# A tuned attention and gated-layer kernel: a first pass over x without the low half, and the first gates placed ahead of the rest of the first layer

## The chip, the cores and the metric

The kernel runs on one core of a Trainium2 chip. The metric is device time in microseconds (us), the median of several executions. Before the change it was 775.09 us (median of 3, 774.56 to 775.32). A profile gives times from the start of its own span, which is some 2 us shorter than the device time.

## The reference, cut to what matters

Two steps on x of 4 batches, 12416 rows, 128 columns. First attention through 32 inducing vectors, twice: the inducing vectors look at x, then x looks at the result `h`. Then a gated feed-forward layer on each row.

```python
def mab(q, kv):                      # attention; scale = 1/sqrt(128)
    a = softmax(scale * q @ kv.T)
    return a @ kv
h = mab(I, x)                        # 32 x 128 per batch
y = mab(x, h)                        # 12416 x 128 per batch
g = y @ w_gate                       # 128 -> 1536
ffn = gelu(g) * (y @ w_val) @ w_out
out = y + sigmoid(y @ w_res) * ffn
```

Since y is a mix of only 32 rows of `h`, the kernel multiplies `h` with the gate and value weights first (called the first layer, `hgv`). A gate is then a product of the attention weights `rt` (32 rows) with `hgv`, followed by a GELU on ScalarE.

## The kernel before: the parts that the change and the argument touch

The first batch has nothing to hide behind: its whole x has to be read before `h`, and `h` is needed for the first gate. Its first pass takes 13 tiles of 1024 rows (the last one short). Each tile is cast to fp16 (`hi`), transposed on TensorE, multiplied with the inducing vectors, put through exp, and summed into the accumulator `acc`, weighted with the exps. In most tiles x is summed as a pair of fp16 numbers, a high and a low half; in five (`whole`) as fp32, as it was loaded.

```python
    for n in range(ntile + 2):
        hi_next(n + 1)                                  # cast of the next tile
        if n < ntile:
            if tiles[n] not in whole:
                convert_lo(0, tiles[n], ve)             # VectorE: x - hi
            turn_pe(0, tiles[n], ve if n in (9, 11, 12) else act)
        if 1 <= n <= ntile:
            ...
            exps("a", 0, n0, n0 + w, bank_v())          # scores and exps
        if n >= 2:
            ...
            if tiles[n - 2] in whole:
                sum_whole(n0, w, n == ntile + 1)        # sums of the exps, VectorE
            accumulate(0, n0, n0 + w, n == 2, n == ntile + 1)
```

Then comes the way from the accumulator to the first gate:

```python
    turn_first_h(0)                       # accumulator -> ht, h transposed
    ...                                   # exps "b": x looks at h, blocks 0 to 32
    exps("b", 0, WIDE, 2 * WIDE, bank_v())          # scores 32 to 64
    exps("b", 0, *later[0], bank_g())
    weights_b(0, 0, 0, half, ve, True)
    first_layer(0, 0, layers[:, :TOK])              # two products, then a VectorE copy
    for j in later[1:]:
        exps("b", 0, *j, bank_g())
    first_layer(0, TOK, layers[:, TOK:])
    finish_h(0)
    layers = bank_v()
    first_layer(0, 2 * TOK, layers[:, :TOK])
    res_layer(0, ve, layers[:, TOK:])               # residual product, same bank
    ...
    act.activation(gel, parts, AC.Gelu, ...)        # trial: loads the GELU table
    for i in range(2):
        pe.matmul(warm, wG[:, :P], wG[:, :TOK], ...)  # two idle products
    # then the plan: G is a gate, P a value product with its multiply, and so on
    plan_first = ["GGGPG VG 5GQ 5Q GQG6 P7G", ...]
```

The softmax here doesn't subtract the row's maximum and nothing guards it: scores larger than these inputs give would overflow.

## Time and profile before

| what | us from the span's start |
|---|---|
| first cast of x to fp16 | 4.83 |
| last full tile landed, its cast starts | 22.20 |
| accumulator copied | 27.90 |
| `ht` ready | 29.68 |
| first gate on ScalarE | 38.12 |
| granted TensorE clock full from ... to ... | 15.7 to 29.4, 32.8 to 36.2, from 49.8 |
| end | 772.7 |

Read it as one chain: the start ends at the first gate, and behind it three engines are full to the end.

### The profile page before, as it was taken

To read this page: it belongs to the slowest core of one execution; us is meant where nothing else is said; L and a number is where in the kernel's file an instruction comes from. 1 tells how busy PE (TensorE), PEld (TensorE's weight loads), DVE (VectorE), ACT (ScalarE), POOL (GpSimd) and SP (SyncE) were. 2 spreads that over 40 slices of the span, in tenths; PEclk is the share of its full clock that TensorE was granted. 3 is DMA by queue.
4 is the path that set the end of the run, shared out by engine and by line. 5 is a ranking of instruction groups with operands and counts; after the bars stand their busy time and mean duration, and the time that the engine had idled before them with its cause. 6 is when DMAs were issued, how large, how long until landed. Compare 5 with 4: busy or idle time off the path is not lost.

```text
span 772.7 us, 23916 instructions
## 1 busy us (share of the span) xinstructions
PE 742.3 (96%) x9593; PEld 433.4 (56%) x9593; DVE 742.4 (96%) x742; ACT 748.4 (97%) x1499; POOL 461.7 (60%) x461
## 2 busy tenths in 40 slices
PE   6899999999999999999999999999999999999997
PEld 5545556565655555565655555566565555555655
DVE  7689999999999999999999999998999999999998
ACT  6599999999999999999999999999999999999997
POOL 0446999712767879723377788952266664533444
PEclk9879999999999999999999999999999999999999
DMA  8323688811054477620035565860005341001101
GB/s 335 124 46 90 161 199 167 174 45 43 29 117 100 125 190 196 151 61 29 29 77 114 111 165 141 208 138 31 28 30 117 87 98 42 38 34 42 43 29 60
DMA packets 118449, 78.16 MB, mean 101 GB/s; under 512 B 96672, under 2 KB 99392, under 8 KB 118336
## 3 DMA queue, kind: packets, MB, share of 16 engines
q1 hardware_dynamic: 118336, 76.62, 38.7%
q8 instruction: 75, 1.23, 0.6%
q14 instruction: 38, 0.31, 0.1%
HBM read 27.87 MB, written 25.43 MB: 69 GB/s over the span
## 4 chain that ended last, share of the span: by engine, by line
PE 48%; ACT 33%; issue 9%; DVE 6%; DMA 2%; POOL 2%; SPq 0%; DVEq 0%; ACTq 0%; POOLq 0%
ACT ge L411 24%; PE f L434 22%; PE g L400 12%; PE v L400 7%; DVE u L405 4%; PE g L442 3%; ACT th L448 3%; ACT at L453 2%; ACT e L172 1%; ACT fe L462 1%; PE g L169 1%; DMA ge<-in_x_dram 1%; DMA rt<-a 1%; DVE lo L124 1%; ACT L172 1%
## 5 line engine op out<-in xcount | busy, mean ns | idle before, releaser
L405 DVE TENSOR_TENSOR u<-ge,v 128x1024 bf16<-128x1024 f32 x584 | 670.9, 1209 | 9.8 <-ACT ge L411 2.6
L411 ACT ACTIVATE ge<-g 128x512 f32<-128x512 f32 x1164 | 605.0, 657 | 5.4 <-PE g L400 2.7
L434 PEld LDWEIGHTS <-u 128*128 128x128 bf16 x4656 | 270.9, 98 | 213.3 <-issue 208.8
L434 PE MATMUL f<-wO,u 128*128 128x128 bf16 x4656 | 374.8, 221 | 3.8 <-DVE th L466 0.7
L400 PE MATMUL g<-rt,hgv 32*128 32x512 f16 x1152 | 336.8, 381 | 8.5 <-DMA rt<-a 0.8
L400 PE MATMUL v<-rt,hgv 32*128 32x512 f16 x1152 | 222.7, 387 | 1.8 <-DVE u L405 1.4
L467 POOL TENSOR_TENSOR at<-at,th 128x512 f32<-128x512 f32 (+1 forms) x99 | 123.7, 1250 | 129.0 <-ACT ge L411 35.5
L400 PEld LDWEIGHTS <-hgv 32*128 32x128 bf16 x2400 | 74.3, 91 | 88.8 <-issue 23.9
L463 POOL TENSOR_TENSOR th<-th,fe 128x512 f32<-128x512 f32 (+1 forms) x33 | 39.7, 1202 | 97.8 <-ACT fe L462 97.8
L337 POOL TENSOR_TENSOR a<-e,z 128x1024 f16<-128x1024 f32 (+1 forms) x48 | 89.8, 1881 | 10.3 <-DMA rt<-a 5.0
L124 POOL TENSOR_TENSOR lo<-xf,hi 128x1024 f16<-128x1024 f32 x36 | 76.9, 2137 | 0.2
L442 PE MATMUL g<-hra,rt 128*128 128x128 f16 x768 | 71.6, 219 | 1.4
L453 ACT ACTIVATE at<-g 128x512 f32<-128x512 f32 (+1 forms) x100 | 63.6, 645 | 0.3
L448 ACT ACTIVATE th<-g 128x512 f32<-128x512 f32 (+1 forms) x100 | 63.2, 644 | 0.5 <-PE g L442 0.2
L442 PEld LDWEIGHTS <-rt 128*128 128x128 f16 x768 | 50.7, 98 | 10.0 <-issue 8.0
L466 DVE SCALAR_TENSOR_TENSOR th<-th,f 128x512 f32<-128x512 f32 (+1 forms) x67 | 45.3, 676 | 3.2 <-PE f L434 1.8
L118 POOL CAST hi<-xf 128x1024 f16<-128x1024 f32 x36 | 37.4, 1038 | 16.6 <-DMA xf<-in_x_dram 16.3
L464 POOL TENSOR_TENSOR at<-at,fe 128x512 f32<-128x512 f32 (+1 forms) x33 | 39.7, 1204 | 0.0
L313 POOL TENSOR_TENSOR a<-e 128x512 f32<-128x512 f32 (+1 forms) x12 | 15.4, 1280 | 21.8 <-ACT e L172 21.8
L169 PEld LDWEIGHTS <-xt 128*128 128x128 f16 x768 | 23.5, 97 | 5.8 <-issue 3.5
L172 ACT ACTIVATE e<-g 128x512 f32<-128x512 f32 (+3 forms) x40 | 21.0, 602 | 3.7 <-PE g L169 3.6
L316 POOL TENSOR_TENSOR a<-a 128x256 f32<-128x256 f32 (+8 forms) x48 | 20.0, 417 | 3.8
(132 smaller groups left out, 262.9 us busy)
## 6 DMA issues: line engine op xcount, KB each, us to landing
out_dram<-at SPq DMA_DIRECT2D x96, 256.0 KB, 2.2
xf<-in_x_dram SPq DMA_DIRECT2D x38, 512.0 KB, 4.5
ge<-in_x_dram SPq DMA_DIRECT2D x10, 512.0 KB, 8.5
rt<-a SPq DMA_TRANSPOSE x48, 3.1
xt<-hi SPq DMA_TRANSPOSE x36, 3.8
ge<-in_moe_w_gate_dram SPq DMA_DIRECT2D x1, 512.0 KB, 9.5
ge<-in_moe_w_val_dram SPq DMA_DIRECT2D x1, 512.0 KB, 9.1
ge<-in_moe_w_out_dram SPq DMA_DIRECT2D x1, 512.0 KB, 4.4
```

The lines of the kernel that those rows point to most:

```text
L124: eng.tensor_tensor(lo[:, :w, :P], xf_t.pop((b, k))[:, :w, :], hi_t[b, k][:, :w, :], AL.subtract)
L337: eng.tensor_tensor(a2[:, :n], ev[:, o:o + n, :].unsqueeze(2).to_broadcast([P, n, Q, M]), z[:, o:o + n].unsqueeze(2).unsqueeze(3).to_broad ...
L400: pe.matmul(*t[n], start=True, stop=True)
L405: ve.tensor_tensor(u[:, :n], ge_t.pop(value)[:, :n], v_t.pop(value)[:, :n], AL.mult)
L411: act.activation(ge_t[i][:, h * TOK:h * TOK + n], gb[:, :n], AC.Gelu, bias=0.0, scale=1.0)
L434: pe.matmul(self.ffn[:, k, :], u_t[self.gi, si][:, o:o + P], wO[:, fc, :], start=first, stop=not self.todo, skip_group_check=True)
L442: pe.matmul(bank[:, k * P:(k + 1) * P], rt_t[self.b, self.k][:, self.j0 + k, :], hra_t[self.b][:, s, :], start=True, stop=True)
L448: act.activation(self.th[:, :self.tw], self.mix(0), AC.Tanh, bias=0.0, scale=0.5)
L453: act.activation(self.at[:, :self.tw], self.mix(1), AC.Copy, bias=0.0, scale=1.0)
L463: po.tensor_tensor(th, th, fe, AL.mult)
L466: ve.scalar_tensor_tensor(th, th, 1.0, f, AL.add, AL.mult)
L467: (ve if self.gi == ngrp - 1 else po).tensor_tensor(at, at, th, AL.add)
```

## The change

Its intent is to shorten the start. In words: all x of the first batch is summed in fp32, so the low half goes; the exps are added up on GpSimd (Pool); the short tile goes last; nine idle products on zeros come first, meant to raise the clock; x is fetched ahead of the inducing vectors; in the second part two first-layer pairs go ahead of scores 32 to 64, and the rest of the first layer goes behind the first three gates. Core of the diff, cuts marked:

```diff
+    WARM = 9
...
-            if b == 0 and k in whole:
-                pe.matmul(o[:, 0:P], e, xf_t[b, k][:, jj, :], start=False, ...)
+            if b == 0:
+                pe.matmul(o[:, 0:P], e, xf_t[b, k][:, jj, :], start=(first and j < j0 + Q), ...)
...
+    def add_up(n0, w):
+        ...
+            po.tensor_tensor(e_of["s"], e_of["s"], e, AL.add)
...
     def first_layer(b, c, bank):
         for r, w in ((slice(0, 64), wG), (slice(64, 128), wV)):
             pe.matmul(bank[r, :], ht_t[b][:, r], w[:, c:c + TOK], start=True, stop=True)
+
+    def first_layer_out(b, c, bank):
         ve.tensor_scalar(hgv_t[b][:, c:c + TOK], bank, parts, None, op0=AL.mult)
...
+    fetch(0, 0, p_ge)
+    fetch(0, 1, p_ge)
     sy.dma_start(ind_f, inducing)
+    ...                                   # tiles 2 to 11, then the short one
+    warm = p_hl.tile(...); ve.memset(warm..., 0.0)
...
+    for i in range(WARM):
+        pe.matmul(wb, warm[:, :P], warm[:, :TOK], start=True, stop=True)
     pe.transpose(i1t_ps[:, :M], ind_f, ident[:M, :M])
...
-            if tiles[n] not in whole:
-                convert_lo(0, tiles[n], ve)
+                add_up(n0, w)
...
+    first_layer(0, 0, layers[:, :TOK])
+    first_layer(0, TOK, layers[:, TOK:])
+    first_layer_out(0, 0, layers[:, :TOK])
+    exps("b", 0, WIDE, 2 * WIDE, bank_v())
...
-    for i in range(2):
-        pe.matmul(warm, wG[:, :P], wG[:, :TOK], start=True, stop=True)
+    def rest_of_first():                  # third pair, residual product, then the copies
+        ...
     plan_first = [
-        "GGGPG VG 5GQ 5Q GQG6 P7G",
+        "GGG!PG VG 5GQ 5Q GQG6 P7G",      # ! calls rest_of_first
```

More of the change, by code (lines that the diff above doesn't have):

```diff
@@ L104, in fetch @@
             xf = p_ge.tile([P, 2 * TOK], FP32, name="ge", tag="ge").rearrange(
+                "p (k c) -> p k c", c=P)
+        elif pool is p_u:
+            xf = p_u.tile([P, 2 * TOK], BF16, name="u", tag="u").bitcast(FP32).rearrange(
                 "p (k c) -> p k c", c=P)
@@ L161, in exps @@
         e = e_t[kind, t0]
-        if kind == "a" and b == 0 and j0 // PRE not in whole:
-            e = e[:, (j0 - t0) * M:(j1 - t0) * M].bitcast(FP16)
-            t0 = j0
         rows = I1T if kind == "a" else ht_t[b][:, 0:M]
@@ L185, in accumulate @@
             e = e_of.pop(("a", b, j))
-            if b == 0 and k in whole:
-                pe.matmul(o[:, 0:P], e, xf_t[b, k][:, jj, :], start=False,
-                          stop=(last and j + Q >= j1), skip_group_check=True)
+            if b == 0:
+                pe.matmul(o[:, 0:P], e, xf_t[b, k][:, jj, :],
+                          start=(first and j < j0 + Q), stop=(last and j + Q >= j1),
+                          skip_group_check=True)
                 continue
@@ L201, in accumulate, with total, finish_h @@
             del acc_t[b]
-    def sum_whole(n0, w, last):
+    def add_up(n0, w):
         e = e_t["a", n0 // WIDE * WIDE][:, n0 % WIDE * M:(n0 % WIDE + w) * M]
-        if not last:
-            if "s" not in e_of:
-                e_of["s"] = e
-            else:
-                s = p_sm.tile([P, PRE * Q * M], FP16, name="a2", tag="a2").bitcast(FP32)[:, :w * M]
-                ve.tensor_tensor(s, e_of["s"], e, AL.add)
-                e_of["s"] = s
-            return
-        for s in (e_of.pop("s"), e):
-            for q in range(0, w, Q):
-                pe.matmul(acc_t[0][:, P:P + 1], s[:, q * M:(q + Q) * M], one,
-                          start=False, stop=False, skip_group_check=True)
-    def finish_h(b):
-        hs = bank_g()
-        pe.matmul(hs[:, 0:P + 1], strips.rearrange("p q m -> p (q m)"), nacc_t.pop(b),
-                  start=True, stop=True)
+        if "s" not in e_of:
+            e_of["s"] = p_sm.tile([P, PRE * Q * M], FP16, name="a2", tag="a2").bitcast(FP32)[:, :w * M]
+            po.tensor_copy(e_of["s"], e)
+        else:
+            po.tensor_tensor(e_of["s"], e_of["s"], e, AL.add)
+    def total(s):
+        n = s.shape[1]
+        for q in range(0, n, Q * M):
+            r = min(Q * M, n - q)
+            pe.matmul(acc_t[0][:r, P:P + 1], s[:, q:q + r], one,
+                      start=False, stop=False, skip_group_check=True)
+    def finish_h(b, hs=None):
+        if hs is None:
+            hs = bank_g()
+            pe.matmul(hs[:, 0:P + 1], strips.rearrange("p q m -> p (q m)"), nacc_t.pop(b),
+                      start=True, stop=True)
         rz = p_h.tile([P, 1], FP32, name="rz1", tag="rz1")
@@ L290, in res_layer @@
     def res_layer(b, eng=act, bank=None):
-        bank = bank_g() if bank is None else bank
-        pe.matmul(bank[:64, :P], ht_t[b][:, :64], wR, start=True, stop=True)
+        if bank is None:
+            bank = bank_g()
+            pe.matmul(bank[:64, :P], ht_t[b][:, :64], wR, start=True, stop=True)
         hra = hra_t[b]
@@ L342, in weights_b, with turned @@
         if by_pe:
-            tps = bank_f().bitcast(FP16).rearrange("p (k c) -> p k c", c=P)
-            for j in range(n):
-                pe.transpose(tps[:, j, :], a2[:, j].rearrange("p q m -> p (q m)"), identF)
-            ve.tensor_copy(rt, tps[:, :n, :])
+            def turned():
+                tps = bank_f().bitcast(FP16).rearrange("p (k c) -> p k c", c=P)
+                for j in range(n):
+                    pe.transpose(tps[:, j, :], a2[:, j].rearrange("p q m -> p (q m)"), identF)
+                ve.tensor_copy(rt, tps[:, :n, :])
+            return turned
         else:
@@ L486 @@
     one = konst.tile([P, 1], FP32, name="one")
-    whole = ()
+    fetch(0, 0, p_ge)
+    fetch(0, 1, p_ge)
     sy.dma_start(ind_f, inducing)
-    tiles = list(range(ntile))
-    if blocks_of(ntile - 1)[1] < PRE:
-        tiles.insert(2, tiles.pop())
-    whole = tuple(tiles[n] for n in (8, 9, 10, 11, 12))
-    for n, k in enumerate(tiles):
-        fetch(0, k, p_x if n in (8, 9) else p_ge)
+    for k in range(2, 8):
+        fetch(0, k, p_ge)
+    for k in range(8, ntile - 2):
+        fetch(0, k, p_x)
+    fetch(0, ntile - 2, p_ge)
+    fetch(0, ntile - 1, p_u)
+    warm = p_hl.tile([P, PRE, P + 2], FP16, name="lo", tag="lo").rearrange("p k c -> p (k c)")
+    ve.memset(warm[:, :TOK].bitcast(FP32), 0.0)
     make_identity(nc, ident)
@@ L508 @@
         ve.tensor_copy(strips[:, q, :], strips[:, 0, :])
+    wb = bank_f()
+    for i in range(WARM):
+        pe.matmul(wb, warm[:, :P], warm[:, :TOK], start=True, stop=True)
     i1t_ps = bank_g()
@@ L536, in weight_cast @@
             eng.tensor_copy(dst, staged.pop(i)[:, :w])
-    for i in range(2):
-        p_ge.tile([P, 2 * TOK], FP32, name="ge", tag="ge")
     for i in range(len(pieces)):
         weight_in(i)
-    def hi_next(n):
-        if n < ntile:
-            convert_hi(0, tiles[n], act if n in (1, 4) else ve)
-    hi_next(0)
-    for n in range(ntile + 2):
-        hi_next(n + 1)
-        if n < ntile:
-            if tiles[n] not in whole:
-                convert_lo(0, tiles[n], ve)
-            turn_pe(0, tiles[n], ve if n in (9, 11, 12) else act)
+    tiles = list(range(ntile))
+    convert_hi(0, 0, ve)
+    for n in range(ntile + 2):
+        if n + 1 < ntile:
+            convert_hi(0, n + 1, act if n == 0 else ve)
+        if n < ntile:
+            turn_pe(0, n, act if n < 10 and n % 2 == 0 or n == ntile - 1 else ve)
         if 1 <= n <= ntile:
-            n0, w = blocks_of(tiles[n - 1])
+            n0, w = blocks_of(n - 1)
             exps("a", 0, n0, n0 + w, bank_v())
+            if n < ntile - 1:
+                add_up(n0, w)
+            if n == ntile - 1:
+                weight_cast(2, act)
         if n >= 2:
-            n0, w = blocks_of(tiles[n - 2])
-            if tiles[n - 2] in whole:
-                sum_whole(n0, w, n == ntile + 1)
+            n0, w = blocks_of(n - 2)
+            if n == ntile:
+                total(e_of.pop("s"))
+                total(e_t["a", n0 // WIDE * WIDE][:, n0 % WIDE * M:(n0 % WIDE + w) * M])
+            if n == ntile + 1:
+                total(e_t["a", n0 // WIDE * WIDE][:, :w * M])
             accumulate(0, n0, n0 + w, n == 2, n == ntile + 1)
-    for i in range(2):
-        weight_cast(i, act)
-    for i in range(2, 5):
-        weight_cast(i, po)
+    weight_cast(0, po)
+    weight_cast(1, po)
+    weight_cast(3, act)
+    weight_cast(4, po)
     turn_first_h(0)
     half = PRE // 2
-    later = [(j0, min(j0 + WIDE // 2, nblk)) for j0 in range(2 * WIDE, nblk, WIDE // 2)]
     exps("b", 0, 0, half, bank_g())
@@ L573 @@
     ones_b(0, 0, half)
+    turned = weights_b(0, 0, 0, half, ve, True)
     exps("b", 0, half, WIDE // 2, bank_g())
@@ L576 @@
     sums_b(0, half, WIDE, po)
-    exps("b", 0, WIDE, 2 * WIDE, bank_v())
-    exps("b", 0, *later[0], bank_g())
-    weights_b(0, 0, 0, half, ve, True)
     layers = bank_v()
     first_layer(0, 0, layers[:, :TOK])
-    for j in later[1:]:
+    first_layer(0, TOK, layers[:, TOK:])
+    first_layer_out(0, 0, layers[:, :TOK])
+    exps("b", 0, WIDE, 2 * WIDE, bank_v())
+    turned()
+    later = [(j0, min(j0 + WIDE // 2, nblk)) for j0 in range(2 * WIDE, nblk, WIDE // 2)]
+    for j in later:
         exps("b", 0, *j, bank_g())
-    first_layer(0, TOK, layers[:, TOK:])
+    first_layer_out(0, TOK, layers[:, TOK:])
     weight_cast(5, po)
-    finish_h(0)
-    layers = bank_v()
-    first_layer(0, 2 * TOK, layers[:, :TOK])
-    res_layer(0, ve, layers[:, TOK:])
     ones_b(0, half, WIDE)
@@ L597 @@
     act.activation(gel, parts, AC.Gelu, bias=0.0, scale=1.0)
-    warm = bank_g()
-    for i in range(2):
-        pe.matmul(warm, wG[:, :P], wG[:, :TOK], start=True, stop=True)
+    def rest_of_first():
+        layers = bank_v()
+        first_layer(0, 2 * TOK, layers[:, :TOK])
+        rs, hs = layers[:, TOK:TOK + P], layers[:, TOK + P:TOK + 2 * P + 1]
+        pe.matmul(rs[:64, :], ht_t[0][:, :64], wR, start=True, stop=True)
+        pe.matmul(hs, strips.rearrange("p q m -> p (q m)"), nacc_t.pop(0), start=True, stop=True)
+        first_layer_out(0, 2 * TOK, layers[:, :TOK])
+        finish_h(0, hs)
+        res_layer(0, ve, rs)
     plan_first = [
-        "GGGPG VG 5GQ 5Q GQG6 P7G",
+        "GGG!PG VG 5GQ 5Q GQG6 P7G",
         "Q6 GQA 10RP 8A1GQR 3P 7Q",
@@ L814 @@
                     emit(None, 1)
+                elif t == "!":
+                    rest_of_first()
                 elif t.isdigit():
```

## The prediction

> **What bounds the kernel now.** I read the page first (engine shares and the forty slices), then the busy time by stretch, then the timeline of the first 60 us. The whole run is a start of 38 us, in which the first batch's attention is worked out, and 734 us of a steady stage in which ScalarE, TensorE and VectorE are all nearly full:
>
> ```profile
> span 772.7 us, 23916 instructions
> PE 742.3 (96%) x9593; PEld 433.4 (56%) x9593; DVE 742.4 (96%) x742; ACT 748.4 (97%) x1499; POOL 461.7 (60%) x461
> PEclk9879999999999999999999999999999999999999
> ```
>
> The reader should see two things: three engines at 96 to 97%, so the steady stage cannot shrink unless its work shrinks (the change leaves it alone); and a granted clock that is low only in slices 2 and 3, just where the start passes into the steady stage. So the change can win only in the start and in the first microseconds behind it. The next view gives busy time by stretch (columns: the stretch, its length, then each engine with its instruction count, the granted TensorE clock, DMA share, GB/s):
>
> ```profile
> 38.12:50.00 11.88, 11.42 (x79) 5.30 (x76) 9.62 (x8) 10.33 (x20) 3.03 (x3) 0.51 0.18 34
> 50.00:62.00 12.00, 11.43 (x123) 5.85 (x120) 11.32 (x11) 11.79 (x26) 6.91 (x8) 1.00 0.18 45
> ```
>
> From the first gate activation (38.12) to 50 the clock is halved and ScalarE is busy 10.33 of 11.88 us: 1.55 us are lost there. From 50 on it is full. The timeline shows the serial end of the start (start us, length us, engine, line, operation, in brackets the idle time and its releaser):
>
> ```profile
> 24.45 1.70 DVE L211 TENSOR_TENSOR a<-a,e 128x256 f32<-128x256 f32 x2
> 24.83 1.04 POOL L536 CAST wG<-ge 128x1024 bf16<-128x1024 f32 x1 [23.19 <-DMA ge<-in_moe_w_gate_dram]
> 26.20 0.61 PE L216 MATMUL f<-one,a 128*128 128x1 f32 x4 [0.24 <-DVE a L211]
> 27.18 0.65 PE L187 MATMUL f<-ge,e 128*32 128x128 f32 x16
> 27.90 0.29 DVE L197 COPY nacc<-f 128x129 f32<-128x129 f32 x1 [1.75 <-PE f L187]
> 29.39 0.29 DVE L250 TENSOR_TENSOR ht<-g,zi 128x128 f16<-128x128 f32 x1
> 34.20 1.28 ACT L597 ACT_TABLE_LOAD   x1
> 35.49 0.20 ACT L597 ACTIVATE gel<-parts 128x1 f32<-128x1 f32 x1
> 36.46 1.03 PE L600 MATMUL g<-wG 128*128 128x512 bf16 x2
> 38.12 3.54 ACT L411 ACTIVATE ge<-g 128x512 f32<-128x512 f32 x7 [2.42 <-issue]
> ```
>
> Read it backwards: ScalarE is ready for gates at 35.69 and idles 2.42 us, because TensorE first does the rest of the first layer, the residual product and two idle products. The inducing result (`ht`) is ready at 29.68, 1.78 us after the accumulator is copied (27.90). The accumulator had waited for the last tile of x, whose fp16 cast starts at 22.20 straight behind its transfer; from 8 to 22 us the DMA engines are busy all the time at 0.37 to 0.43 MB per us. So the start is: transfers to 22.20, a tail of 5.70 to 27.90, 1.78 to `ht`, 8.44 to the first gate.
>
> [...] of the two VectorE adds at 24.45 the first took 0.41 us, the second began at 24.96 inside GpSimd's 1.04 us cast and took 1.19. [...] from the mean clock of each microsecond I work out changes at 29.36, 32.78, 36.18 and 49.84, which are 3.4, 3.4 and four times 3.4 us apart. Eight transposes took 1.03 us up to 13.6 us and 0.62 from 16.6 on, so the array was also cold until about 15.5, although the records show 1.00 there. [...]
>
> **The change part by part.**
>
> (1) First pass over x. Removed: eight VectorE subtractions for the low half (seven of 1.22 us and a short one), about 9 us, and the low/high fp16 product pairs. Every tile now costs VectorE one cast of 0.69 us, and every other tile a 0.68 us copy out of PSUM as well: 1.03 us a tile. Before, cast and subtraction ran at 1.73 us a tile from 12 to 19 us. TensorE pays 0.55 (eight transposes, start to start), 0.36 (scores) and 0.58 (sixteen fp32 passes), as tiles 20 to 23 us ran before: 1.32 us a tile at full clock. ScalarE pays 0.38 and every other tile 1.02: 0.9. A tile of 0.52 MB takes 1.28 us at 0.41 MB per us, so transfers and TensorE now tie. Hence the idle products: cold, a tile would cost TensorE about twice that, 2.6 us. Nine of 512 columns at half clock last about 9 x 0.43 = 3.8 us[...], over before the first cast at 4.8.
>
> GpSimd's ten adds of 128x256 fp32 cost some 0.7 us each (0.73 in its like at L316). [...]
>
> (2) The order of transfers. x starts 0.45 us sooner (0.75, no longer behind the inducing load), the short tile's 512-byte rows go last, and the weights wait for TensorE's sums. In the 7.7 MB moved by 22.2 us were 1.3 MB of weights, 3 us worth; part of that remains ahead of x, as eight transfers are still kept outstanding. I put the last full tile at 21.3 (20.3 to 22): 0.9 us gained.
>
> (3) The tail. Cast 0.69, transposes 0.62, copy 0.69, scores 0.36, exp 0.38, with 0.1 between each: 3.2 us. Then ScalarE casts a weight (1.04) before the short tile's exp (0.19), beside TensorE's sums (0.5 for the totals, 0.65 for the tile): 1.3 us, then 0.5 for the short tile. Together 5.0 against 5.70. Gone are the two late VectorE adds held up by GpSimd's cast, which kept TensorE from 25.9 to 26.2, and half of the totals. 0.7 us gained; accumulator copy at about 26.3.
>
> (4) From `ht` to the first gate. The exps need 3.8 us of ScalarE, the table and its trial 1.5. But two first-layer pairs (0.4 to 0.5 us each) now stand before scores 32 to 64, so ScalarE waits for those about 1.2 us: 0.4 to start, 1.3 for the first three exps, 1.3 of wait, 1.0 + 0.6 + 0.6 + 0.2, then 1.5: 6.9 us. Three gates are issued behind the last score and need only the first 512 columns, so they are done before the table is. 6.9 against 8.44: 1.5 us gained.
>
> (5) Behind the first gate. The rest of the first layer, the normalisation and residual copies (VectorE 0.75 + 0.16 + 0.35 + 0.28 + 0.28 = 1.8 us) now fall beside the first gates. The first gated product starts perhaps 0.8 us later relative to the first gate than before, costing ScalarE some 0.4. Against this, TensorE loses the idle stretch at 35 to 36.2[...]; I give half a chance that the clock holds, worth half of 1.55, so 0.7. Net 0.3.
>
> Sum: 0.9 + 0.7 + 1.5 + 0.3 = 3.4 us; rounded up to 3.6, as the lighter VectorE should let hidden waits go too.
>
> **The rivals.**
> (a) [...] Then TensorE runs cold up to 12 us, lies some three tiles behind and ends its sums at 26.5 to 27.5; with (4) that leaves about 2 us of gain, 773. For it: 36 to 50 us, where the array stayed cold for four windows although shown busy 96%. [...]
> (b) [...] gain about 2, 773.
> (c) The transfers end much sooner, because nothing but x is queued: 6.4 MB at 0.41 end at about 19.5, and the warm clock holds through the first gates. Gain 6 to 7, 768.5. Against: TensorE at 1.32 us a tile cannot end its part before 21.
> (d) The gain of the start is given back in the steady stage, by a buffer freed late. I see no such link: all weights arrive earlier, and ScalarE is full from 50 us on.
>
> **Range and chances.** The middle is 775.09 - 3.6 = 771.5 us. (a) and (b) set the upper edge at 774, (c) the lower at 769. Faster by over 2% would need 15.5 us, almost half of the whole start, while transfers alone need 19: 1%. Slower by 2% would need a new wait repeated in the steady stage: 1%.
>
> **What would show it.** Right: first gate activation at 34 to 36 us; accumulator copy at 25.5 to 27; no transfer of x outstanding after 22; transposes of 0.62 us by about 9 us; casts of 0.69 us with few above 1 us; ScalarE going from the trial activation straight into gates; equal ScalarE time from there to the end. Wrong: transposes of 1.03 us beyond 12 us (a), casts of 1.2 us and more (b), a first gate before 33 us (c), or a span from first gate to end that differs from 734.6 by over 2 us (d).

In (5), 0.7 us is the author's estimate, half of the 1.55 us that ScalarE lost from 38.12 to 50. Of rival (a), that TensorE stays at half clock in the first tiles, the "four windows" are 4 x 3.41 us, from 36.18 to 49.84. Of rival (b), that VectorE and GpSimd hold each other up, the gain of about 2 us was the author's estimate (its 1.2 us is near the 1.19 us that VectorE's add inside GpSimd's cast took). The 2.6 us of a cold tile in (1) is an estimate too: twice the 1.32 us, for a clock of about one half (0.51 from 38.12 to 50).

## More of the kernel before

All differences here are of a few tenths of a per cent, so each experiment was timed in several rounds beside the kernel before.

What the start gains, the end gains, if nothing gives it back. The prediction shows the lines for this. Two lines of the timeline that it does not show become important later (columns: start, length, engine, line, operation, and in brackets the idle time and its releaser):

```profile
4.83 0.69 DVE L118 CAST hi<-ge 128x1024 f16<-128x1024 f32 x1 [1.72 <-DMA ge<-in_x_dram]
36.21 0.31 PE L292 MATMUL v<-wR,ht 128*64 128x128 bf16 x1 [1.24 <-DVE hgv L266]
```

The first cast waits for its tile of x alone. And TensorE was idle for 1.24 us ahead of the residual product, just before the first gate. That product goes to the same bank (a buffer that TensorE's products are written into) as the last first-layer pair and was issued after the VectorE copy that reads that pair; the profile names this copy (L266) as what ended the wait, and in the run that issues the product ahead of the copy the wait is gone.

## The result, and the profile after

| | before | after |
|---|---|---|
| median (lowest to highest, executions) | 774.83 (774.15 to 775.32, 4) | 771.83 (771.35 to 772.86, 4) |
| ratio | | 0.9964, 95% interval 0.9950 to 0.9978 |

That is 3.0 us, within 2%. Ratios here and below are the mean time of one kernel's fast runs over that of the other's of the same rounds, so not quite the ratio of the medians. The page of the kernel after:

```profile
span 769.6 us, 23941 instructions
PE 744.0 (97%) x9602; PEld 433.1 (56%) x9602; DVE 736.1 (96%) x737; ACT 744.0 (97%) x1494; POOL 470.4 (61%) x464
PEclk9889999999999999999999999999999999999999
```

The steady stage is as it was, and slices 2 and 3 are still low. VectorE has lost only 6.3 us of 742.4, since the steady stage is nearly all of its work. The stations of the start, in us:

| | before | after | lead |
|---|---|---|---|
| first cast | 4.83 | 6.45 | -1.62 |
| last full tile's cast | 22.20 | 21.15 | 1.05 |
| accumulator copied | 27.90 | 27.22 | 0.68 |
| `ht` ready | 29.68 | 29.00 | 0.68 |
| first gate | 38.12 | 35.63 | 2.49 |
| 100th gate | 97.19 | 94.40 | 2.79 |
| end | 772.68 | 769.58 | 3.10 |

The timeline of the kernel after, first 15 us (columns as above):

```profile
1.20 4.02 PE L520 MATMUL f<-lo 128*128 128x512 f16 x9 [1.20 <-DVE lo L506]
1.67 0.42 SPq L498 DMA_DIRECT2D u<-in_inducing_dram  x1
6.09 0.21 PE L522 MATMUL g<-ident,u 32*128 32x32 f32 x1 [0.87 <-DMA u<-in_inducing_dram]
6.34 0.19 DVE L523 CAST I1T<-g 128x32 f16<-128x32 f32 x1 [3.83 <-PE g L522]
6.45 0.69 DVE L122 CAST hi<-ge 128x1024 f16<-128x1024 f32 x1
7.19 1.07 PE L144 MATMUL g<-identF,hi 128*128 128x128 f16 x16 [0.89 <-DVE hi L122]
9.16 1.01 PE L144 MATMUL g<-identF,hi 128*128 128x128 f16 x8
11.34 0.90 PE L144 MATMUL g<-identF,hi 128*128 128x128 f16 x8
12.93 0.62 PE L144 MATMUL g<-identF,hi 128*128 128x128 f16 x8
```

Read it from the top. The records show full clock from 5.13 us, after the nine idle products from 1.20 (without them, below, only from 12.31). But the load of the inducing vectors, now third in the queue, lands only at 5.96 us, though the first tile of x had landed at 4.49. On VectorE the copy of the inducing vectors is placed ahead of the first cast of x, and they ran in that order (6.34, then 6.45), so the cast is 1.6 us later than before, and TensorE, done with its idle products at 5.22, has next to nothing to do until 7.19. The busy time in two stretches between changes of the clock, 3.41 us apart, shows the price (columns: stretch, length, each engine's busy time with its instructions, granted clock, DMA share, GB/s):

```profile
5.13:8.54 3.41, 1.37 (x18) 1.03 (x17) 1.25 (x3) 1.74 (x2) 0.00 (x0) 1.00 0.91 342
8.54:11.96 3.42, 3.03 (x47) 2.58 (x48) 2.23 (x4) 2.02 (x4) 0.81 (x2) 0.50 1.02 419
```

In the stretch of full clock TensorE was busy 1.37 us, and the next 3.42 us were at half clock. Tiles start at 9.16, 11.34 and 12.93 there, 2.18 and 1.59 us apart. From 12.93 on they start about 1.32 us apart (12.93, 14.25, 15.57, 16.89, 18.20, 19.64, 20.96, 22.28): TensorE is now the bound, with no room to catch up. The end of the start:

```profile
21.15 0.69 DVE L122 CAST hi<-ge 128x1024 f16<-128x1024 f32 x1
22.28 0.62 PE L144 MATMUL g<-identF,hi 128*128 128x128 f16 x8
23.99 0.42 PE L187 MATMUL f<-xf,e 128*32 128x128 f32 x8 [0.54 <-issue]
27.22 0.29 DVE L198 COPY nacc<-f 128x129 f32<-128x129 f32 x1 [3.59 <-PE f L187]
28.71 0.29 DVE L253 TENSOR_TENSOR ht<-g,zi 128x128 f16<-128x128 f32 x1
32.12 1.02 ACT L172 ACTIVATE e<-v 128x1024 f32<-128x1024 f32 x1 [1.42 <-PE v L169]
34.23 1.28 ACT L607 ACT_TABLE_LOAD   x1
35.63 3.51 ACT L419 ACTIVATE ge<-g 128x512 f32<-128x512 f32 x7
```

The last full tile is cast by 21.84, but its transposes wait for TensorE until 22.28; a further 0.54 us are lost ahead of 23.99 to a stall of TensorE marked "issue", for which the profile shows no releaser (the last experiment is about it; in the repeat of this kernel it took 1.24 us). Behind `ht` ScalarE waits 1.42 us for scores 32 to 64, which two first-layer pairs now precede, and then goes from the table straight into the gates.

### The profile page after: what moved, and what is told of

It is laid out like the page before. It is cut to its first block, busy times and chain, and to the rows that moved or that the text cites. A ratio compares the mean times of both kernels' runs of the same rounds, so it can differ in the third digit from the quotient of the medians.

```text
span 769.6 us, 23941 instructions
## 1 busy us (share of the span) xinstructions
PE 744.0 (97%) x9602; PEld 433.1 (56%) x9602; DVE 736.1 (96%) x737; ACT 744.0 (97%) x1494; POOL 470.4 (61%) x464
## 4 chain that ended last, share of the span: by engine, by line
PE 48%; ACT 34%; issue 10%; DVE 5%; POOL 2%; DMA 1%; DVEq 0%; SPq 0%; ACTq 0%; POOLq 0%
ACT ge L419 25%; PE f L442 21%; PE g L408 11%; PE v L408 7%; DVE u L413 5%; PE g L450 3%; ACT th L456 3%; ACT at L461 3%; ACT fe L470 1%; ACT e L172 1%; PE g L169 1%; PE f L187 1%; PE g L144 1%; DVE th L474 1%; POOL lo L128 1%
```

## The experiments

Twelve runs followed (eleven variants and a repeat of the changed kernel), all with correct results. Unless the text says otherwise the diff is against the kernel after.

### The load of the inducing vectors first again

Theory: its place in the queue delays the first cast, opens the idle stretch of TensorE and loses the clock. Rival: the first pass is bound by TensorE, by transfers or by casts drawn out beside GpSimd's adds anyway, and the delay is absorbed.

```diff
+    sy.dma_start(ind_f, inducing)
     fetch(0, 0, p_ge)
     fetch(0, 1, p_ge)
-    sy.dma_start(ind_f, inducing)
```

> The changed kernel with the inducing load put back ahead of x. My theory: in the changed kernel the first cast stands behind the copy of the inducing matrix on VectorE (6.34), whose load took 4.3 us behind two tiles of x, so TensorE idles from 5.22 to 7.19 and the clock falls at 8.54. With the load first: first cast of tile 0 at about 5.0 instead of 6.45, first transposes at about 5.7 instead of 7.19. If the clock then holds to 12 us, the first gate comes 1.0 to 1.5 us sooner (34.1 to 34.6) and the time falls by as much; if it falls all the same, 0.3 to 0.5 us sooner. Rival (the start hangs on the transfers of x): first gate unchanged at 35.4 to 35.8.

Measured: median 770.73 us (770.42 to 773.33, 6 executions), ratio 0.9958 (0.9945 to 0.9971). Its timeline:

```profile
5.59 0.68 DVE L122 CAST hi<-ge 128x1024 f16<-128x1024 f32 x1
6.33 0.62 PE L144 MATMUL g<-identF,hi 128*128 128x128 f16 x8 [0.89 <-DVE hi L122]
16.49 1.24 DVE L122 CAST hi<-xf 128x1024 f16<-128x1024 f32 x1 [2.03 <-DMA xf<-in_x_dram]
```

The transposes are at full speed from the first tile; the clock, up at 5.30, held to 29.2. So the theory holds in the trace as to the clock. The first cast missed its expected 5.0, though: on TensorE the inducing vectors' transpose stands behind the idle products, which end at 5.22, and the cast stands behind the copy of that transpose. The accumulator was copied at 26.18, the first gate came at 34.28, 1.35 us earlier than with the change as it stands. Of the 1.04 us at the accumulator only 0.38 lie in the pass itself (last full tile's transposes at 21.90 rather than 22.28); 0.54 is the stall ahead of 23.99, which did not come here, and another run with the load first (the first tile ahead, below) has one of 0.59. A gain in time is not shown: the median is about 1 us lower, by the ratios it is 0.5 us, and the intervals overlap. The third line shows what bounds the pass once TensorE is not: a transfer, for which VectorE waited 2.03 us, and then a cast that took 1.24 instead of 0.69 us beside an add of GpSimd, for which TensorE waited 0.70 us.

### No idle products

```diff
-    WARM = 9
+    WARM = 0
```

> The changed kernel without its nine idle products. My theory: they warm the array only for the first two tiles, since the clock falls again at 8.54, so leaving them out costs 0.5 to 1.0 us: first transposes at 1.03 us, clock up at about 12 as before, first gate 36.1 to 36.6, time up by 0.5 to 1.0. The prediction on record saw them as what keeps TensorE three tiles ahead: then first gate at 37 to 38 and 1.5 to 2.5 us lost.

Measured: median 773.55 us (771.82 to 775.40, 6), ratio 0.9989 (0.9975 to 1.0003). In the profiled run the clock rose only at 12.31; the accumulator was copied at 28.19, 1.0 us later than after, and the first gate came at 36.61, also 1.0 later. Half of this is the first pass (last full tile's transposes at 22.76 rather than 22.28), the other half a longer stall of TensorE behind it (1.06 rather than 0.54 us; the changed kernel's own repeat has 1.24). So in these two traces the idle products are worth about 0.5 us in the first pass. The median lost 1.7. In the profiled execution a further 1.5 us went between the first gate and the end (735.43 us against 733.95), with the clock at half until 49.86; others ran at a low mean clock too (775.40 at 0.983, against 771.82 at 0.990).

### The rest of the first layer ahead of the gates again

This undoes the last words of the change, the gates ahead of the rest, but keeps the split that issues the residual product before the copies.

```diff
+    rest_of_first()
     plan_first = [
-        "GGG!PG VG 5GQ 5Q GQG6 P7G",
+        "GGGPG VG 5GQ 5Q GQG6 P7G",
```

> The changed kernel with the rest of the first layer, the residual product and the normalisation put back ahead of the first three gates. Theory A (the table load hides that work, what was gained was the wait on VectorE between the products and the two idle products behind them): first gate 35.5 to 36.0 as in the changed kernel, time within 0.4 us of it. Theory B (the prediction's part 4, the order itself is worth 1.5 us): first gate 36.8 to 37.3, time 1.2 to 1.7 us longer.

Measured: median 771.29 us (770.57 to 772.84, 5), ratio 0.9958 (0.9946 to 0.9970), so no worse than the change. The profile fell in its slowest execution; there the clock rose only at 13.35, and it was at half from 27.00 to 37.24, so all stations are late, but the distance that matters can be read:

```profile
30.73 0.29 DVE L253 TENSOR_TENSOR ht<-g,zi 128x128 f16<-128x128 f32 x1
36.26 1.28 ACT L607 ACT_TABLE_LOAD   x1
36.69 0.61 PE L408 MATMUL g<-rt,hgv 32*128 32x512 f16 x2
37.66 4.00 ACT L419 ACTIVATE ge<-g 128x512 f32<-128x512 f32 x8
```

From `ht` (31.02) to the first gate are 6.64 us, against 6.63 with the change. (The like at half clock all the way is the run without idle products, with the order of the change: also 6.64. At full clock all the way, in the repeat below, that order took 6.26.) The gates' products (36.69) are under way while the table is still being loaded. Placing the gates ahead of the rest is worth nothing: ScalarE could not have taken them sooner.

### The exps added on VectorE

```diff
-            po.tensor_copy(e_of["s"], e)
+            ve.tensor_copy(e_of["s"], e)
         else:
-            po.tensor_tensor(e_of["s"], e_of["s"], e, AL.add)
+            ve.tensor_tensor(e_of["s"], e_of["s"], e, AL.add)
```

> The changed kernel with the running sum of the exps added on VectorE instead of GpSimd. Theory A (TensorE sets the pace at 1.32 us a tile[...]): tiles still 1.32 us apart, first gate within 0.3 us of 35.63, time within 0.4 us. Theory B[...]: casts of 0.69 us throughout, and first gate 0.5 to 1.0 us sooner.

(What is measured: in the changed kernel one cast took 1.22 us and one 0.80, beside GpSimd's adds, the other full ones 0.68 to 0.70, some of them beside an add too (17.42, 18.63). Theory B is that such casts cost time.)

Measured: median 772.80 us (772.57 to 773.32, 5), ratio 0.9978 (0.9965 to 0.9990). Accumulator at 28.58, first gate at 36.60, 1.4 and 1.0 us later. Neither theory had this. All casts but that of the last full tile (1.10 us, beside a weight cast on GpSimd) take 0.69 us now, and still tiles are on average 1.55 us apart from 12.83 to 22.15:

```profile
14.82 0.43 DVE L211 TENSOR_TENSOR a<-a,e 128x256 f32<-128x256 f32 x1 [0.83 <-ACT e L172]
15.16 0.69 DVE L122 CAST hi<-ge 128x1024 f16<-128x1024 f32 x1
```

VectorE stood 0.83 us waiting for ScalarE's exp, so that it could do the add; the cast of the next tile comes behind the add in its queue, and the transposes follow the cast. It is not the work of the adds (0.43 us each) but the wait that they bring in ahead of the cast. On GpSimd that wait holds up no cast, and the longer cast beside an add (one of 1.22 us among those of the kernel after) is hidden there behind TensorE's 1.32 us a tile; with the load first, above, it was not.

### The kernel before with its residual product moved, nothing else

Here the diff is against the kernel before. The bank's products are issued ahead of the copy, and the two idle products at the end are dropped.

```diff
     first_layer(0, 2 * TOK, layers[:, :TOK])
+    pe.matmul(layers[:64, TOK:TOK + P], ht_t[0][:, :64], wR, start=True, stop=True)
+    first_layer_out(0, 2 * TOK, layers[:, :TOK])
     res_layer(0, ve, layers[:, TOK:])         # no longer issues the product
...
-    warm = bank_g()
-    for i in range(2):
-        pe.matmul(warm, wG[:, :P], wG[:, :TOK], start=True, stop=True)
```

> The kernel before with one thing altered: the residual product issued straight behind the first-layer products, before VectorE's copy of them, and no idle products behind it. Nothing of the first pass is touched. Theory A (part 4's gain is that wait of 1.24 us and the idle products, not the order of the gates): from the inducing result to the first gate 6.3 to 6.8 us instead of 8.44, first gate at 36.0 to 36.5, time 1.5 to 2.2 us under before. Theory B (order needed): first gate stays above 37.5.

Measured: median 772.27 us (771.31 to 774.63, 6), ratio 0.9974 (0.9958 to 0.9989): 2.4 us under the 774.66 of the kernel before in these rounds. Its timeline:

```profile
28.73 0.29 DVE L250 TENSOR_TENSOR ht<-g,zi 128x128 f16<-128x128 f32 x1
33.58 1.28 ACT L604 ACT_TABLE_LOAD   x1
34.19 0.22 PE L594 MATMUL v<-wR,ht 128*64 128x128 bf16 x1
34.98 1.55 ACT L414 ACTIVATE ge<-g 128x512 f32<-128x512 f32 x3
```

The residual product no longer waits, and the first gate follows the table (33.58 to 34.86) at once. `ht` was ready at 29.02, so `ht` to first gate fell from 8.44 to 5.96 us: 2.48 us from a reordering of a few lines. The change as a whole got 1.81 there; the 0.67 between them I put down to its two first-layer pairs ahead of scores 32 to 64, behind which ScalarE waits 1.42 us. The old order, below, gives nearly the same 0.61, but the repeat of the changed kernel varies by 0.37, so the size is rough; at half clock all the way it is 6.64 (no idle products) against 6.02 (old order), 0.62. (0.66 of this run's earlier first gate lies ahead of `ht` and is another matter: its first pass is that of the kernel before, but its clock rose at 15.12 rather than 15.71.) The interval of this ratio holds those of the changed kernel (0.9964, and 0.9971 in its repeat). So the times don't show that all the rest of the change adds anything to these few lines.

### Scores 32 to 64 ahead of the first-layer pairs

```diff
     sums_b(0, half, WIDE, po)
+    exps("b", 0, WIDE, 2 * WIDE, bank_v())
     layers = bank_v()
     first_layer(0, 0, layers[:, :TOK])
     first_layer(0, TOK, layers[:, TOK:])
     first_layer_out(0, 0, layers[:, :TOK])
-    exps("b", 0, WIDE, 2 * WIDE, bank_v())
```

> The changed kernel with the scores of blocks 32 to 64 issued ahead of the two first-layer pairs. Theory: ScalarE's wait of 1.42 us for those scores (32.12) goes; from the inducing result to the first gate 5.6 instead of 6.63 us, first gate about 34.6, time 0.8 to 1.1 us shorter than the changed kernel's. Rival: the hgv copies then come too late for the gates and the gain is under 0.3.

Measured: median 773.27 us (771.24 to 774.41, 6), ratio 0.9981 (0.9965 to 0.9997). A miss: `ht` at 29.50 to first gate at 36.07 is 6.57 us, not 5.6. The wait of 1.42 us did not go; it moved:

```profile
31.51 1.02 ACT L172 ACTIVATE e<-v 128x1024 f32<-128x1024 f32 x1 [0.32 <-PE v L169]
33.47 1.08 ACT L172 ACTIVATE e<-g 128x512 f32<-128x512 f32 x2 [0.94 <-PE g L169]
```

Scores 32 to 64 now wait 0.32 us, but those behind them wait 0.94, as the pairs still stand ahead of the last scores and the array is at half clock there (29.62 to 33.04 in this run).

### Both, with the first tile ahead of the inducing vectors

The load first and scores 32 to 64 first together, and the first tile's cast and transposes issued ahead of the inducing vectors' transpose, so that a late inducing load cannot hold them.

```diff
+    sy.dma_start(ind_f, inducing)                # first again
...
+    convert_hi(0, 0, ve)
+    convert_hi(0, 1, act)
+    turn_pe(0, 0, act)
     i1t_ps = bank_g()
     pe.transpose(i1t_ps[:, :M], ind_f, ident[:M, :M])
...                                               # and scores 32 to 64 first
```

> Both of the above on the changed kernel: inducing load first, the first cast and transposes issued ahead of the inducing transpose, and scores 32 to 64 ahead of the first-layer pairs. First cast at 4.9, first transposes 5.6, clock held from about 5 to 27; accumulator copy about 26; first gate 33.0 to 33.5; time 769.3 to 770.2. If transfers are the bound once TensorE starts sooner, the accumulator copy stays at 26.2 as in the run with the inducing load first.

Measured: median 771.11 us (770.09 to 774.24, 6), ratio 0.9963 (0.9946 to 0.9981). First cast 4.77, but accumulator at 26.33 and first gate at 34.45, against 26.18 and 34.28 with the load moved alone. The earlier first tile bought nothing up to a transfer that both had to wait for (casts at 16.45 and 16.49). Behind it this run led by 0.56 us (last full tile's transposes at 21.34 rather than 21.90, as the cast at 16.45 took 0.73 us instead of 1.24), and the stall of TensorE, 0.59 us here, took that back. The expected 33.0 to 33.5 for the first gate was missed by about as much as the scores' order had failed to give.

### The array kept filled

On top of that, idle products wherever TensorE has a pause: ten at the start, two and three around the making of `ht`, and two at each `w` in the plan.

```diff
+    idle(2, wb)
     turn_first_h(0)
+    idle(3, wb)
...
-        "GGG!PG VG 5GQ 5Q GQG6 P7G",
+        "wGGG!wPwG VwG w5GQ 5Q GQG6 P7G",
```

> The same, with idle products also in TensorE's idle stretches between the accumulator and the inducing result, and between the first gates. Theory (the half clock from 36 to 46 costs ScalarE about 1.8 us there): the clock stays at 1.0 from about 5 us to the end, first gate 32.7 to 33.3, 20th gate activation 11.5 to 12.0 us behind the first instead of 13.0, time 767.7 to 768.8. Rival: idle products only lengthen TensorE's queue, the clock falls all the same, and the time is that of the run without them or longer.

Measured: median 769.0 us (768.49 to 772.79, 6), ratio 0.9942 (0.9922 to 0.9962). In the profiled run the clock was full from 6.11 to 763.9 of 766.9 us, the first gate came at 33.87, and 20 gates took 11.98 us. Two executions of the six, with lower mean clocks (771.01 at 0.994, 772.79 at 0.993), were slower; where the clock was low in them is not shown, as they were not profiled. As a trial, three idle products after the first tile's transposes and two after the second's were added:

```diff
     turn_pe(0, 0, act)
+    idle(3, wb)
...
+        if n == 1:
+            idle(2, wb)
```

> The best version so far with five more idle products, three behind the first tile's transposes and two behind the second's. [...] all executions lie within 768.3 to 769.8. Rival: the scatter has another cause and stays; or the added products delay the first tiles and cost 0.3 us or more in every execution.

Measured: median 768.66 us (768.26 to 768.81, 5), ratio 0.9928 (0.9915 to 0.9941). This is the best version: 5.5 us under the kernel before in the same rounds (774.2), and 3.0 under the changed kernel in its repeat below (771.62). Of its page, the clock:

```profile
PEclk9999999999999999999999999999999999999999
```

No slice is low. The first 20 gates, as one stretch in the kernel before, the changed kernel and this one:

```profile
38.12:51.27 13.15, 12.69 (x97) 6.21 (x93) 10.21 (x9) 11.40 (x22) 3.03 (x3) 0.55 0.16 32
```

```profile
35.63:48.67 13.04, 12.06 (x92) 5.39 (x90) 11.70 (x14) 11.23 (x23) 3.81 (x7) 0.61 0.17 33
```

```profile
33.57:45.55 11.98, 11.20 (x99) 4.85 (x98) 11.03 (x14) 10.91 (x24) 4.59 (x8) 1.00 0.18 36
```

With full clock (1.00 rather than 0.61) the 20 gates take 13.04 - 11.98 = 1.06 us less, and the first gate is 35.63 - 33.57 = 2.06 earlier: together 3.1, what the medians show.

### The changed kernel again, and with the old order of the second part

A repeat of the changed kernel, unaltered:

> The changed kernel once more, beside the two below on one chip. Time 771.3 to 773, 2.0 to 3.2 us under before; the executions should scatter by 1 to 2 us[...].

Measured: median 771.62 us (770.86 to 773.07, 5), ratio 0.9971 (0.9959 to 0.9983), so the result stands. In its profile the clock did not fall at 29 us, but it fell at 8.65 and at 35.96 again; `ht` to first gate took 6.26 us. Its accumulator came at 28.04 and its first gate at 36.08, 0.8 and 0.45 us later than in the first profile of the same kernel, mostly by its stall of 1.24 us. So a difference of under a microsecond between two kernels' stations needs its cause in the lines.

Then the changed kernel with scores, first-layer pairs and `turned()` in the order of the kernel before:

```diff
+    later = [...]
+    exps("b", 0, WIDE, 2 * WIDE, bank_v())
+    exps("b", 0, *later[0], bank_g())
+    turned()
     layers = bank_v()
     first_layer(0, 0, layers[:, :TOK])
-    first_layer(0, TOK, layers[:, TOK:])
     first_layer_out(0, 0, layers[:, :TOK])
...
+    for j in later[1:]:
+        exps("b", 0, *j, bank_g())
+    first_layer(0, TOK, layers[:, TOK:])
```

> The changed kernel with the scores and first-layer products of the second pass in the order of the kernel before (scores to block 80, then the first pair, then the last scores, then the second pair), the gates left as changed. Theory: the new order costs ScalarE its wait of 1.42 us; from the inducing result to the first gate 5.9 to 6.1 us as in the kernel before without its wait and idle products, instead of 6.63; time 0.4 to 0.8 us under the changed kernel's. Rival: the wait only moves, as when the one group of scores was moved, and it stays at 6.5 to 6.7.

Measured: median 772.18 us (771.02 to 774.82, 6), ratio 0.9981 (0.9966 to 0.9996). The distance came out as expected, 31.57 to 37.59 = 6.02 us, but in the slowest of its executions, with the clock at half from 26.34 to 50.23. Two of the six executions ran at a mean clock of 0.981 (774.64 and 774.82). A gain in time is not shown.

### The idle products cut into four

This asks what the stall of TensorE ahead of 23.99 belongs to. In seven runs (the changed kernel, its repeat, and those with no idle products, the rest first, scores first, the first tile ahead, and the old order) a stall of 0.54 to 1.24 us stands ahead of product number 346 of TensorE, counted from 0. It is the same number without the nine idle products, although that is another place of the program. Ahead of each a 16 KB transfer of the kind "instruction" starts, in the changed kernel at 21.43; the DMA view of 21.30 to 21.60 has it as (packets, MB, share):

```profile
q8 instruction: 1, 0.02, 21.4%
```

The nine idle products were cut into 36 of 128 columns: the same work, 27 more products.

```diff
-    for i in range(WARM):
-        pe.matmul(wb, warm[:, :P], warm[:, :TOK], start=True, stop=True)
+    for i in range(4 * WARM):
+        pe.matmul(wb[:, :P], warm[:, :P], warm[:, :P], start=True, stop=True)
```

> The changed kernel with its nine idle products of 512 columns cut into 36 of 128 columns: the same array time, but 27 more TensorE products ahead of the first pass. It asks what the unexplained stall of TensorE near 23.5 us belongs to. In the traces of the changed kernel, its repeat and four variants, the stall (0.54 to 1.24 us, marked issue) stands ahead of product number 346 counted from 0, even where nine idle products were left out, and its end is 2.49 to 2.56 us after a 16 KB transfer of kind instruction starts (21.43 in the changed kernel). Theory A: [...] Then a stall, if there is one, is again ahead of product 346, now 27 products earlier in the program (in the sum of the last tile but one or at the transposes of the last full tile), with its end 2.5 us after the start of such a transfer, and none is left in the middle of the sum of the last tile but one's successor, where it is in the changed kernel. Theory B: it belongs to that place of the program (the bank, the operands or the weights' transfers at that time). Then it stays ahead of the same product, now number 373. Time: within 0.7 us of the changed kernel either way, 771 to 772.5.

(Theory A: the stall goes by the product's number.)

Measured: median 771.58 us (770.80 to 773.65, 4), ratio 0.9970 (0.9942 to 0.9999): the changed kernel's time. But the stall is gone from its place; the sum that was cut in two by it runs through:

```profile
23.17 0.65 PE L187 MATMUL f<-xf,e 128*32 128x128 f32 x16
```

The accumulator is copied at 26.65 rather than 27.22, though the pass before it is no faster (last full tile's transposes at 22.43 rather than 22.28). So the stall does not belong to the place in the program; it goes by the number of the product. Product 346 now starts at 22.21, 2.65 us after the instruction transfer (19.55), and does not stall; the seven stalls ended 2.49 to 2.56 us after theirs. Two runs without a stall had 2.40 and 2.41, so this distance alone does not tell a stall. Two more numbers go with the count. The changed kernel's page counts 75 of these transfers to 19204 products and weight loads of TensorE, on average one to 256. And where the first pass ran early, TensorE stalled at product 220 too, which is 126 products and their weight loads, 252 instructions, before 346: with the load first for 0.43 us (16.68), 2.38 us after a transfer, and with the array kept filled for 0.24 and 0.25 us. How such a transfer and the stall hang together is not shown; no run changed the transfers alone.

## Why the prediction was right, and where its steps were not

The time (771.5 predicted, 771.83 measured) and the range were right. The five parts, predicted against the lead in the traces:

| part | predicted gain | measured |
|---|---|---|
| (1), (2) last full tile | 0.9, at 21.3 | 1.05, at 21.15 |
| (3) tail to the accumulator copy | 0.7 (5.0 us) | -0.37 (6.07 us) |
| (4) `ht` to first gate | 1.5 (6.9 us) | 1.81 (6.63 us) |
| (5) behind the first gate | 0.3 | 0.61 |
| sum | 3.4, rounded up to 3.6 | 3.10 |

**The mis-sized term is (3).** It gave the tail 5.0 us, with the transposes straight behind the last cast; it took 6.07. The prediction had put the idle products "over before the first cast at 4.8". That took the first cast from the kernel before, although the change moves the inducing load behind two tiles of x and VectorE takes its copy first; the cast came at 6.45. The changed order on each engine, which could be read before any run, had this in it; what it does not show is how long the load takes. And its idle products, begun at 1.20, end at 5.22, so even with the load first the cast behind them came at 5.59. The clock fell again, TensorE lay behind from tile 2 on, and at 1.32 us a tile it never caught up, so the last transposes began 0.44 us after their cast ended; with the stall of 0.54 us this makes 0.98 of the 1.07 by which the tail exceeded 5.0. The experiment with the load first shows the delay and the lost clock, but not that they made the tail long: its accumulator at 26.18 is near the predicted 26.3 because its last full tile was cast at 20.53 rather than 21.3; its tail is 5.65, and its last transposes begin 0.69 us behind the cast's end. No run with the new first pass had a tail of 5.0; the shortest is 5.34, without the stall. What failed is the assumption that TensorE, tied with the transfers at 1.32 us a tile, would be free when the last cast ends. The stall goes by the count of instructions, not by places in the program, and went away with 27 products more ahead of it; its cause is not shown.

One sum of part (1) is wrong as written: 0.55 + 0.36 + 0.58 is 1.49, not 1.32. The 1.32 itself is right, as the trace has it: 0.46, 0.28 and 0.58 from start to start (12.93, 13.39, 13.67, 14.25).

**Part (4) has the right size for partly the wrong reason.** The prediction explained the gain by gates that are issued behind the last score. The rest of the first layer put ahead of the gates again costs nothing (6.64 us, at no better clock). What paid was the removed wait of the residual product, with the two idle products behind it: 2.48 us when done alone. The predicted wait of "about 1.2 us" for scores behind two pairs was there, 1.42 us, and it is what takes some 0.6 of the 2.48 back.

**Part (5)** held in size. The lead grows by 0.61 to 3.10 at the end. The clock did fall at 35.85, so the coin fell on the wrong side, but it came back at 46.09 rather than at 49.84.

That the sum came so near is in part luck: (3) was 1.07 too high, and the other three parts were 0.15, 0.31 and 0.31 too low.

**The rivals.** (a), a cold array in the first tiles, came true in part: in the profiled run the clock was up at 5.13, but at half from 8.54 to 11.96. In the run with the rest first, whose first pass is the same, it came up only at 13.35 (accumulator at 28.73). Transposes took 1.01 us at 9.16, and were at 0.62 from 12.93. Where the idle products are left out, the start is 1.0 us longer, half of it by the stall. (b), casts drawn out beside GpSimd: one of 1.22 us and one of 0.80 appeared, harmless behind TensorE here. (c) and (d) did not come: the first gate was at 35.63, and from there to the end are 733.95 us against 734.56.

What the prediction had not foreseen at all is the scatter. Executions of one kernel lie 0.75 to 4.3 us apart here, and the slower ones mostly have the lower mean clock; in the best version, with the array kept filled, five lie within 0.55 us. So the difference of 3.0 us between before and after is well shown, but single steps of half a microsecond had to be read from distances in the traces rather than from medians.

## What to carry to other kernels

Before moving a small load back in a queue, look for an engine that has its consumer placed ahead of something urgent: here a 16 KB load held up the cast of a tile that had landed 1.96 us earlier. Idle products at the start paid little here (about 0.5 us) while a pause followed them; short runs of them in every pause of TensorE took a further 2.1 us off (771.11 to 769.00 in the same rounds), and five more of them the scatter (768.66). And when a product is issued into a bank beside another one, issue it before the copy that reads the bank: that alone, with two idle products dropped, took 2.4 us off the kernel before.

## What the traces show of the clock, the table load and the queues

- In the profiles the changes of the granted clock are multiples of 3.41 us apart, and counted back in such steps they lay 1.47 to 3.11 us behind the span's start. In the kernel before and the changed one TensorE was shown busy 1.37 to 2.80 of the 3.41 us ahead of each fall at the start, so none of these falls followed an idle stretch of that length. In the changed kernel the clock fell after stretches in which TensorE was busy 1.37, 2.28 and 2.80 of 3.41 us, and held after 2.87; but with the load first it held after 2.02, and in the repeat after 2.17. In the kernel before it did not rise after the stretch from 39.60, mostly of the gates' 32-row products, that was shown busy throughout (3.42 of 3.42 us). So the busy share of a profile does not decide it. After nine products on zeros the clock was up at 5.13 us, without them at 12.31; but in one run with them (the rest first) only at 13.35. Eight transposes took 1.01 us at half clock and 0.62 at full clock.
- In the changed kernel the load of the GELU table took 1.28 us, and the trial activation behind it began 1.29 us after the load had begun (34.23 and 35.52).
- The inducing vectors took 1.7 us from issue to landing in front of x, and 4.3 us behind two tiles of 512 KB.
- Seven runs had a stall of TensorE of 0.54 to 1.24 us, each ending 2.49 to 2.56 us after a 16 KB transfer of the kind "instruction" had begun, with a DMA share of 1.06 to 1.08 from 20.5 to 25 us. It stood ahead of the same number of TensorE's products in all seven. What ties the two together is not shown.
